# Moving a skipped program from the end of the instruction streams to a place ahead of the last five output tiles

## The chip, the core and the metric

The kernel runs on one core of a Trainium2 chip. The core has five engines, each with an instruction stream of its own: PE (TensorE, matrix products), ACT (ScalarE), DVE (VectorE), POOL (GpSimd) and SP (SyncE, which here only issues transfers). They are tied together by semaphores alone. The metric is the device time of one execution in microseconds. Before the change the median of three runs was 339.82 us (339.38 to 341.15).

## The reference

A sliding-window attention (window 64, 8 batches, 8 heads, 576 positions, head size 64) is followed by a SwiGLU block over the 4608 resulting rows of width 512, with an inner width of 1536:

```python
scores = scale * np.matmul(q, k.transpose(0, 1, 3, 2))
mask = (rel >= 0) & (rel < window)
scores = np.where(mask, scores, -1000000000.0)
scores = scores - np.max(scores, axis=-1, keepdims=True)
attn = np.exp(scores)
attn = attn / (np.sum(attn, axis=-1, keepdims=True) + 1e-09)
...
x = np.ascontiguousarray(attn_out.transpose(0, 2, 1, 3)).reshape(B * S, H * D)
...
g = x @ w_gate
silu = g * (1.0 / (1.0 + np.exp(-g)))
val = x @ w_val
return (silu * val @ w_out).astype(np.float32)
```

## The kernel before

**Tiles and stages.** The rows are taken in 36 chunks of 128 for the attention and in 9 groups of 512 for the SwiGLU block. For a chunk, `T` or `TD` transposes queries and keys, `S` makes the scores and their exponentials, `A` multiplies by the values and divides by the sums, and `X` or `XD` transposes the result into `xT`. For a group `c` and one of twelve inner slices `f`, `F(c, f)` makes four matmuls with the gate weights (call them G) into one PSUM bank and four with the value weights (V) into another; ACT takes the tanh of G (L546), DVE makes `uu` (L548) and then `hT` (L550). `O(c, u)` makes twelve matmuls of `hT` with the output weights (L564) for one tile of 128 output rows, ACT copies the bank to `ost` (L576), and SP stores it (L579). `O_last` does the very last tile in three column pieces (L594), so that its copies (L312 on ACT, L314 on DVE) and stores (L602) are small. The order of all this is written out by hand in `build`. The F matmuls of group 8 are interleaved with the output tiles of group 7: `O(7, u)` stands behind the eighth matmul group of each `u`, but `O(7, 3)` (`late`) stands behind F(8, 11). The stream of PE thus ends with F(8, 9), F(8, 10), F(8, 11) and then five output tiles: O(7, 3), O(8, 0), O(8, 1), O(8, 2) and `O_last`.

**Banks.** The G and V of one F take the next two of four banks; a bank may be written again when the reader of its last content is done. V of F(8, 11) therefore waits for the `hT` of F(8, 9). This wait is a semaphore that DVE raises, carried by the first weight load of that V.

**Two programs.** The exponentials are taken without subtracting a row maximum. `judge` looks, in four steps, whether the sums of all rows are within bounds: steps 0 to 2 (inside group 8) make a flag in SBUF, and step 3 loads it into a register on each engine (L624, `reg_load`). If the flag is not zero, a second program, made by `general`, computes the whole output again in a slower and general way. With the inputs here the flag is zero and that program is skipped.

**The recorder.** All operations are recorded in one `_Graph`. `emit` finds the waits that each operation needs and plays the list into the five streams. For each engine `run` plays the operations up to the mark `cut`, then the branch `If_ne(reg, 0)` with the general program behind it, and on SP the waits until all transfers have landed (`landed`, L148). The streams then meet in the closing barrier of the block (L162): each engine drains, POOL gathers the five signals and releases all.

So each of the streams runs: usual program, branch (L155), general program (skipped), closing barrier. By the listing of the built program, the usual part of PE has 3515 matrix products (each a weight load and a matmul) and the general part 4184.

Of the kernel before, what the change touches and what calls it, by code (L numbers as in the profile page):

```python
# [30 lines left out]
class _Graph:  # L31


    LANES = {"pool": 16, "sp": 16, "act": 8}

    def __init__(self, nc):
        self.nc = nc
        self.ops = []
        self.writers = {}
        self.readers = {}  # L40
        self.cut = None
        self.regs = {}

    def op(self, eng, fn, reads=(), writes=(), dma=False, after=()):
        deps = {o.i: (o, "sync") for o in after}
# [14 lines left out]
            self.readers[k] = []  # L60
        return o

    def general_from_here(self):
        self.cut = len(self.ops)

    def emit(self):
        nc = self.nc
        engines = ["pe", "act", "dve", "pool", "sp"]
        seen = {e: {} for e in engines}
        npos = {e: 0 for e in engines}  # L70
        ndma = {e: 0 for e in engines}
        lanes = {}
        plan = {e: [] for e in engines}
        usual = None
        for o in self.ops:
            if o.i == self.cut:
                usual = dict(lanes)
            e = o.eng
            clock = seen[e]
            waits = []  # L80

            def need(d):
                key = ("dma", d.i) if d.dma else d.eng
                val = 1 if d.dma else d.pos
                if clock.get(key, 0) >= val:
                    return
                waits.append(d)
                d.inc = True
                for k2, v2 in d.clock.items():
                    if clock.get(k2, 0) < v2:  # L90
                        clock[k2] = v2

            deps = sorted(o.deps, key=lambda x: -x[0].i)
            for d, kind in deps:
                if kind != "sync" and d.eng == e and not d.dma and (e == "pe" or kind != "raw") and not o.dma and e != "pool":
                    continue
                need(d)
            if o.dma:
                nl = self.LANES[e]
                o.lane = (e, ndma[e] % nl)  # L100
                o.occ = ndma[e] // nl
                ndma[e] += 1
                prev = lanes.get(o.lane)
                if prev is not None:
                    need(prev)
                lanes[o.lane] = o
            npos[e] += 1
            o.pos = npos[e]
            o.clock = dict(clock)
            if o.dma:  # L110
                o.clock[("dma", o.i)] = 1
            else:
                o.clock[e] = o.pos
            plan[e].append((o, waits))
        cnt = {e: 0 for e in engines}
        for o in self.ops:
            if not o.dma and o.inc:
                cnt[o.eng] += 1
                o.count = cnt[o.eng]
        sem = {e: nc.alloc_semaphore("c_" + e) for e in engines if e != "sp"}  # L120
        for lane in sorted(lanes):
            sem[lane] = nc.alloc_semaphore("d_%s%d" % lane)

        def target(d):
            if d.dma:
                return d.lane, 16 * (d.occ + 1)
            return d.eng, d.count

        def play(eng, e, steps, level):
            for o, waits in steps:  # L130
                want = {}
                for d in waits:
                    k, v = target(d)
                    want[k] = max(want.get(k, 0), v)
                for k, v in want.items():
                    if level.get(k, 0) < v:
                        level[k] = v
                        eng.wait_ge(sem[k], v)
                last = o.fn(eng)
                if o.dma:  # L140
                    last.then_inc(sem[o.lane], 16)
                elif o.inc:
                    last.then_inc(sem[e], 1)

        def landed(eng, on):
            for o in on.values():
                k, v = target(o)
                eng.wait_ge(sem[k], v)  # L148

        def run(eng, e):  # L150
            level = {}
            with eng.register("general_" + e) as reg:
                self.regs[e] = reg
                play(eng, e, [x for x in plan[e] if x[0].i < self.cut], level)
                with eng.If_ne(reg, 0):  # L155
                    play(eng, e, [x for x in plan[e] if x[0].i >= self.cut], level)
                    if e == "sp":
                        landed(eng, lanes)
                if e == "sp":
                    landed(eng, usual)  # L160

        with nc.Block() as block:  # L162
            block.gpsimd(lambda x: run(x, "pool"))
            block.tensor(lambda x: run(x, "pe"))
            block.vector(lambda x: run(x, "dve"))
            block.scalar(lambda x: run(x, "act"))
            block.sync(lambda x: run(x, "sp"))


class _Kernel:  # L170
# [10 lines left out]
    def __init__(self, nc, q, k, v, wg, wv, wo, out):  # L181
        self.nc, self.q, self.k, self.v = nc, q, k, v
        self.wg, self.wv, self.wo, self.out = wg, wv, wo, out
        self.g = _Graph(nc)
        self.alloc()

    def alloc(self):
# [37 lines left out]
        self.ps = [nc.alloc_psum_tensor("ps%d" % i, [128, 512], F32) for i in range(8)]  # L225
        self.rot = {"f": ([0, 1, 2, 3], 0), "a": ([4, 5, 6, 7], 0)}
        self.n_s = 0
        self.stores = {}
        self.kb = [sb("kb%d" % i, 192, F32) for i in range(3)]
        self.ms = sb("ms", H * 192, F32)[:, :].rearrange("p (h k) -> p h k", h=H)  # L230
        self.mx = sb("mx", H, F32)
# [321 lines left out]
    def O(self, c, u, mid=None, kind="a"):  # L553
        g = self.g
        ih = c % self.NH
        hT = self.hT[ih]
        io = (4 * c + u) % self.NO
        ost = self.ost[io]
        OB, ok = self.bank(kind)

        def part(f0, f1):
            def pe(e):
                for f in range(f0, f1):
                    r = e.matmul(OB[:, :], hT[:, f, 128 * u:128 * u + 128], self.Wo[:, f, :],  # L564
                                 start=(f == 0), stop=(f == NF - 1))
                return r

            g.op("pe", pe, reads=[("hT", ih, f) for f in range(f0, f1)] + [("Wo", f) for f in range(f0, f1)], writes=[ok])

        if mid is None:  # L570
            part(0, NF)
        else:
            part(0, 8)
            mid()
            part(8, NF)
        g.op("act", lambda e: e.activation(ost[:, :], OB[:, :], ACTF.Copy), reads=[ok], writes=[("ost", io)])  # L576
        r0 = 512 * c + 128 * u
        was = self.stores.get((c, u), [])
        self.stores[c, u] = [g.op("sp", lambda e: e.dma_start(self.out[r0:r0 + 128, :], ost[:, :]),  # L579
                                  reads=[("ost", io)], dma=True, after=was)]  # L580

    def O_last(self, c, u):
        g = self.g
# [5 lines left out]
        for c0, c1, eng, q in ((0, 256, "act", "sp"), (256, 384, "act", "sp"), (384, 512, "dve", "act")):  # L589
            OB, ok = self.bank("a")  # L590

            def pe(e, OB=OB, c0=c0, c1=c1):
# [5 lines left out]
            g.op("pe", pe, reads=[("hT", ih, f) for f in range(NF)] + [("Wo", f) for f in range(NF)], writes=[ok])  # L598
            d = ost[:, c0:c1]
            self.move(eng, d, OB[:, 0:c1 - c0], [ok] + ([("ost", io)] if c0 else []), [("osth", c0)] + ([("ost", io)] if c0 == 0 else []))  # L600
            self.stores.setdefault((c, u), []).append(
                g.op(q, lambda e, d=d, c0=c0, c1=c1: e.dma_start(self.out[r0:r0 + 128, c0:c1], d), reads=[("osth", c0), ("ost", io)], dma=True))  # L602

    def judge(self, step):

# [9 lines left out]
        elif step == 2:  # L615
            bank, bk = self.bank("f")
            n = bank[0:1, 0:8 * NCH]
            g.op("pe", lambda e: e.matmul(n, self.ones[:, 0:1], ok, start=True, stop=True), reads=["ones", "ok"], writes=[bk])
            g.op("dve", lambda e: e.tensor_reduce(self.low[0:1, :], n, mybir.AxisListType.X, ALU.min), reads=[bk], writes=["low"])
            g.op("dve", lambda e: e.tensor_scalar(self.flag[0:1, :], self.low[0:1, :], 127.5, None, ALU.is_lt),  # L620
                 reads=["low"], writes=["flag"])
        else:
            for eng in ("pe", "act", "dve", "pool", "sp"):
                g.op(eng, lambda e, eng=eng: e.reg_load(g.regs[eng], self.flag[0:1, 0:1]), reads=["flag"])  # L624

    def init_general(self):
        g = self.g
# [81 lines left out]
    def general(self):  # L709


        self.g.general_from_here()
        self.banks("a", [4, 5, 6, 7])
        self.banks("f", [0, 1, 2, 3])
        self.init_general()
        for n in range(NCH):
# [6 lines left out]
            if n % 4 == 3:  # L723
                for f in range(NF):
                    self.F(n // 4, f)
                for u in range(4):
                    self.O(n // 4, u)

    def build(self):
        W = lambda a, b: (self.load_w("g", a, b), self.load_w("v", a, b))  # L730
# [124 lines left out]
                 (2, 0, 0): 12, (2, 1, 0): 13, (2, 1, 2): 14, (2, 2, 1): 15, (2, 3, 0): 16}  # L855
        for n in range(17, NCH):
            place[(n - 5) // 4, (n - 5) % 4, 0] = n
        judged = {(0, 0): 0, (0, 2): 1, (1, 1): 2}
        for c in range(1, NFC):
            for u in range(int(c == 1), 4):  # L860
                late = c == NFC - 1 and u == 3
                for s in range(3):
# [12 lines left out]
                    if c == NFC - 1 and (u, s) in judged:  # L875
                        self.judge(judged[u, s])
                if late:
                    self.O(c - 1, u)
        for u in range(3):
            self.O(NFC - 1, u)  # L880
            if u == 1:
                self.judge(3)
        self.O_last(NFC - 1, 3)
        self.general()
        self.g.emit()


def bass_sliding_window_causal__then__ffn_swiglu_block_kernel(
# [39 lines left out]
```

## Time and profile before

| what | value |
|---|---|
| median of three runs | 339.82 us (339.38 to 341.15) |
| profiled execution, device time | 338.61 us |
| span of that execution, first to last instruction | 337.0 us |
| mean granted TensorE clock | 0.997 |
| PE busy | 320.4 us (95%) |
| DVE, ACT, POOL busy | 215.6, 140.1, 110.8 us |
| end of the last output tile's copy on DVE | 331.6 us after the start of the span |

Times of the profile are microseconds from the start of the span. Line numbers (L155) are those of the kernel before. PEld is the weight load of PE, which runs beside the matmuls. Names with a q (PEldq, ACTq, SPq) are instructions that an engine's sequencer handles by itself: branches, loads of a register, waits, drains and the issue of transfers; the page does not count them as busy. "q8 instruction" and "q14 instruction" are transfers that bring instructions.

### The profile page before, as it was taken

To read this page: it belongs to the slowest core of one execution; us is meant where nothing else is said; L and a number is where in the kernel's file an instruction comes from. 1 tells how busy PE (TensorE), PEld (TensorE's weight loads), DVE (VectorE), ACT (ScalarE), POOL (GpSimd) and SP (SyncE) were. 2 spreads that over 40 slices of the span, in tenths; PEclk is the share of its full clock that TensorE was granted. 3 is DMA by queue.
4 is the path that set the end of the run, shared out by engine and by line. 5 is a ranking of instruction groups with operands and counts; after the bars stand their busy time and mean duration, and the time that the engine had idled before them with its cause. 6 is when DMAs were issued, how large, how long until landed. Compare 5 with 4: busy or idle time off the path is not lost.

```text
span 337.0 us, 8375 instructions
## 1 busy us (share of the span) xinstructions
PE 320.4 (95%) x3478; PEld 165.7 (49%) x3515; DVE 215.6 (64%) x481; ACT 140.1 (42%) x256; POOL 110.8 (33%) x141
## 2 busy tenths in 40 slices
PE   8889989999999999999999999999999999999993
PEld 3657557554444444444444444444444444444442
DVE  5658798476666866666666666666666665555600
ACT  2655764444444444444444444444444422223321
POOL 7999993553545432353333330000000000000000
PEclk9999999999999999999999999999999999999998
DMA  9999999999999999999999999334331111000022
GB/s 169 152 189 173 164 197 158 156 168 166 156 174 173 172 174 171 157 152 134 125 119 117 130 133 118 78 75 77 79 78 49 49 49 47 32 31 34 31 93 71
DMA packets 169517, 40.21 MB, mean 119 GB/s; under 512 B 155904, under 2 KB 164992, under 8 KB 169472
## 3 DMA queue, kind: packets, MB, share of 16 engines
q0 software_dynamic: 117312, 18.36, 77.1%
q1 hardware_dynamic: 50976, 20.66, 32.5%
q10 hardware_dynamic: 1184, 0.59, 0.7%
q8 instruction: 29, 0.48, 0.6%
q14 instruction: 16, 0.13, 0.1%
HBM read 37.75 MB, written 9.44 MB: 140 GB/s over the span
## 4 chain that ended last, share of the span: by engine, by line
PE 85%; DMA 4%; POOL 4%; DVE 2%; issue 2%; ACT 1%; SPq 0%; POOLq 0%
PE ps L540 51%; PE ps L564 26%; PE ps L475 4%; DMA qT<-qn 2%; PE ps L426 2%; DMA Wv<-in_moe_w_val_dram 2%; POOL va L357 1%; PE ps L594 1%; POOL Wg L363 1%; DVE uu L548 1%; POOL qn L295 1%; POOL kn L295 1%; PE ps L382 0%; POOL Wv L363 0%; DVE pt L441 0%
## 5 line engine op out<-in xcount | busy, mean ns | idle before, releaser
L548 DVE SCALAR_TENSOR_TENSOR uu<-sig,ps 128x512 bf16<-128x512 bf16 (+2 forms) x122 | 76.1, 623 | 82.4 <-ACT sig L546 82.1
L540 PE MATMUL ps<-xT,Wv 128*128 128x512 bf16 (+2 forms) x487 | 113.3, 355 | 0.8 <-DMA Wv<-in_moe_w_val_dram 0.7
L540 PE MATMUL ps<-xT,Wg 128*128 128x512 bf16 (+2 forms) x456 | 106.5, 353 | 6.6 <-issue 4.8
L564 PE MATMUL ps<-Wo,hT 128*128 128x512 bf16 x417 | 95.5, 379 | 0.3 <-issue 0.2
L546 ACT ACTIVATE sig<-ps 128x512 bf16<-128x512 f32 (+2 forms) x122 | 66.9, 549 | 60.4 <-PE ps L540 59.8
L550 DVE SCALAR_TENSOR_TENSOR hT<-uu,ps 128x512 bf16<-128x512 bf16 (+2 forms) x122 | 76.3, 625 | 4.8 <-PE ps L540 0.6
L540 PEld LDWEIGHTS ps<-xT,Wv 128*128 128x128 bf16 x488 | 47.0, 98 | 47.6 <-DMA Wv<-in_moe_w_val_dram 1.0
L564 PEld LDWEIGHTS ps<-Wo,hT 128*128 128x128 bf16 x420 | 41.0, 98 | 48.9
L540 PEld LDWEIGHTS ps<-xT,Wg 128*128 128x128 bf16 x488 | 43.7, 98 | 41.9 <-ACT xT L516 0.8
L295 POOL DMA_DIRECT2D qn<-in_q_dram x38 | 35.2, 944 | 84.7 <-DMA qT<-qn 83.3
L576 ACT ACTIVATE ost<-ps 128x512 f32<-128x512 f32 x35 | 20.9, 597 | 95.1 <-PE ps L564 92.2
L436 ACT ACTIVATE pt<-ps 128x512 bf16<-128x512 f32 x72 | 38.9, 595 | 22.0 <-PE ps L426 22.0
L357 POOL DMA_DIRECT2D va<-in_v_dram x40 | 37.2, 941 | 0.9 <-issue 0.6
L295 POOL DMA_DIRECT2D kn<-in_k_dram x38 | 35.4, 937 | 3.7 <-DMA Wo<-in_moe_w_out_dram 3.7
L493 DVE TENSOR_TENSOR xb<-ps,rc 128x256 bf16<-128x256 f32 x72 | 30.6, 424 | 2.5
L441 DVE TENSOR_TENSOR pt<-pt,mask 128x512 bf16<-128x512 bf16 x64 | 24.1, 416 | 0.2 <-ACT pt L436 0.2
L475 PE MATMUL ps<-va,pt 64*64 64x65 bf16 x1088 | 22.9, 197 | 0.6
L475 PEld LDWEIGHTS ps<-va,pt 64*64 64x64 bf16 x1088 | 15.0, 106 | 15.8 <-issue 11.0
L490 DVE RECIPROCAL rc<-ps 128x4 f32<-128x4 f32 x72 | 12.5, 174 | 8.8 <-PE ps L475 8.8
L426 PE MATMUL ps<-qT,kT 64*64 64x64 bf16 (+1 forms) x864 | 15.9, 201 | 0.6 <-DMA qT<-qn 0.6
L426 PEld LDWEIGHTS ps<-qT,kT 64*64 64x64 bf16 x864 | 12.6, 108 | 2.7 <-issue 1.1
L343 PE MATMUL ps<-wz 128*128 128x512 bf16 x17 | 6.9, 573 | 1.4 <-DVE wz L257 1.2
(50 smaller groups left out, 67.3 us busy)
## 6 DMA issues: line engine op xcount, KB each, us to landing
out_dram<-ost SPq DMA_DIRECT2D x35, 256.0 KB, 2.5
va<-in_v_dram POOLq DMA_DIRECT2D x32, 128.0 KB, 11.0
qn<-in_q_dram POOLq DMA_DIRECT2D x30, 128.0 KB, 11.8
kn<-in_k_dram POOLq DMA_DIRECT2D x30, 128.0 KB, 11.1
Wo<-in_moe_w_out_dram POOLq DMA_DIRECT2D x2, 768.0 KB, 15.1
Wg<-in_moe_w_gate_dram POOLq DMA_DIRECT2D x5, 256.0 KB, 8.1
Wv<-in_moe_w_val_dram POOLq DMA_DIRECT2D x5, 256.0 KB, 8.8
fk<-in_k_dram SPq DMA_DIRECT2D x1, 512.0 KB, 4.9
```

The lines of the kernel that those rows point to most:

```text
L295: self.g.op("pool", lambda e, d=d, a=a: e.dma_start(d, a), writes=ks, dma=True)
L357: g.op("pool", lambda e, d=d, a=a: e.dma_start(d, a), writes=ks, dma=True)
L426: r = e.matmul(sv[h][o:o + 64, c, q0:q1], self.kT[ps, c, kk:kk + 64], qT[ps, c, q0:q1], start=not biased, stop=not biased or c == 3 and kk ...
L436: g.op("act", lambda e, po=po, si=si: e.activation(po, si, ACTF.Exp, scale=SCALE), reads=[bk], writes=[pk])
L441: "dve", lambda e: e.tensor_tensor(po, po, m, ALU.mult), reads=[pk, "mask"], writes=[pk]))
L475: r = e.matmul(av[half][ws, j, :], pt[ks, h, ws], vv[ks, h, 0:65], start=key == q[0], stop=key == q[-1])
L493: g.op("dve", lambda e, xo=xo, rb=rb, a=av[half]: e.tensor_tensor(xo, a[:, :, 0:64], rb, ALU.mult), reads=[bk, ("rc", ir)], writes=[("xb", ...
L540: r = e.matmul(bank[:, 0:n], W[:, kk, f * 128:f * 128 + 128], xT[:, kk, t0:t1], start=(kk == 0), stop=(kk == NK - 1))
L546: g.op("act", lambda e: e.activation(sig[:, 0:n], G[:, 0:n], ACTF.Tanh, scale=0.5), reads=[gk], writes=[("sig", i)])
L548: g.op("dve", lambda e: e.scalar_tensor_tensor(uu[:, 0:n], sig[:, 0:n], 1.0, G[:, 0:n], ALU.add, ALU.mult), reads=[("sig", i), gk], writes ...
L550: g.op("dve", lambda e: e.scalar_tensor_tensor(hT[:, f, t0:t1], uu[:, 0:n], 0.5, V[:, 0:n], ALU.mult, ALU.mult), reads=[("uu", i), vk], wr ...
L564: r = e.matmul(OB[:, :], hT[:, f, 128 * u:128 * u + 128], self.Wo[:, f, :], start=(f == 0), stop=(f == NF - 1))
```

## The change

The operations of the usual and of the general program are recorded in two graphs, each with semaphores of its own. A new class `_Program` plays them: on each engine the usual program up to `general_at`, then the branch with the general program behind it, and then the rest of the usual program. `general_at` is set ahead of O(7, 3), so the last five output tiles stand behind the skipped program in each stream. Inside the branch, a gate on each side makes all five engines wait for one another; with the flag at zero neither gate is executed. The loads of the flag into registers (`judge(3)`) move from behind O(8, 1) to behind O(7, 2). The chaining of stores of the same rows (`stores`, `after=was`) goes, since the general program now stores first.

```diff
-    def general_from_here(self):
-        self.cut = len(self.ops)
...
+class _Program:
+    def __init__(self, nc, usual, general, at):
+        self.nc, self.usual, self.general, self.at = nc, usual, general, at
+        self.regs = {}
+
+    def emit(self):
+        nc, usual, general, at = self.nc, self.usual, self.general, self.at
+        usual.plan()
+        general.plan()
+        gates = [nc.alloc_semaphore("gate%d" % i) for i in range(2)]
+        end = 1 << 30
+
+        def gate(eng, i):
+            eng.drain().then_inc(gates[i], 1)
+            eng.wait_ge(gates[i], 5)
 
         def run(eng, e):
-            level = {}
             with eng.register("general_" + e) as reg:
                 self.regs[e] = reg
-                play(eng, e, [x for x in plan[e] if x[0].i < self.cut], level)
+                usual.play(eng, e, 0, at)
                 with eng.If_ne(reg, 0):
-                    play(eng, e, [x for x in plan[e] if x[0].i >= self.cut], level)
                     if e == "sp":
-                        landed(eng, lanes)
+                        usual.landed(eng, at)
+                    gate(eng, 0)
+                    general.play(eng, e, 0, end)
+                    if e == "sp":
+                        general.landed(eng, end)
+                    gate(eng, 1)
+                usual.play(eng, e, at, end)
                 if e == "sp":
-                    landed(eng, usual)
+                    usual.landed(eng, end)
...
     def general(self):
-        self.g.general_from_here()
+        usual, self.g = self.g, _Graph(self.nc, "g")
...
+        self.program = _Program(self.nc, usual, self.g, self.general_at)
+        self.program.emit()
...
-        judged = {(0, 0): 0, (0, 2): 1, (1, 1): 2}
+        judged = {(0, 0): 0, (0, 2): 1, (1, 1): 2, (2, 1): 3}
...
                 if late:
+                    self.general_at = len(self.g.ops)
                     self.O(c - 1, u)
         for u in range(3):
             self.O(NFC - 1, u)
-            if u == 1:
-                self.judge(3)
         self.O_last(NFC - 1, 3)
         self.general()
-        self.g.emit()
```

More of the change, by code (lines that the diff above doesn't have):

```diff
@@ L34, with __init__ @@
     LANES = {"pool": 16, "sp": 16, "act": 8}
-    def __init__(self, nc):
-        self.nc = nc
+    ENGINES = ["pe", "act", "dve", "pool", "sp"]
+    def __init__(self, nc, name):
+        self.nc, self.name = nc, name
         self.ops = []
@@ L40, in __init__ @@
         self.readers = {}
-        self.cut = None
-        self.regs = {}
     def op(self, eng, fn, reads=(), writes=(), dma=False, after=()):
@@ L61, in op, with plan @@
         return o
-    def general_from_here(self):
-        self.cut = len(self.ops)
-    def emit(self):
-        nc = self.nc
-        engines = ["pe", "act", "dve", "pool", "sp"]
+    def plan(self):
+        engines = self.ENGINES
         seen = {e: {} for e in engines}
@@ L72, in emit @@
         lanes = {}
-        plan = {e: [] for e in engines}
-        usual = None
+        self.steps = {e: [] for e in engines}
         for o in self.ops:
-            if o.i == self.cut:
-                usual = dict(lanes)
             e = o.eng
@@ L113, in emit @@
                 o.clock[e] = o.pos
-            plan[e].append((o, waits))
+            self.steps[e].append((o, waits))
         cnt = {e: 0 for e in engines}
@@ L119, in emit @@
                 o.count = cnt[o.eng]
-        sem = {e: nc.alloc_semaphore("c_" + e) for e in engines if e != "sp"}
+        self.sem = {e: self.nc.alloc_semaphore(self.name + "c_" + e) for e in engines if e != "sp"}
         for lane in sorted(lanes):
[L122 to L148, printed above, removed]
+            self.sem[lane] = self.nc.alloc_semaphore(self.name + "d_%s%d" % lane)
+        self.level = {e: {} for e in engines}
+    def target(self, d):
+        if d.dma:
+            return d.lane, 16 * (d.occ + 1)
+        return d.eng, d.count
+    def play(self, eng, e, i0, i1):
+        level = self.level[e]
+        for o, waits in self.steps[e]:
+            if not i0 <= o.i < i1:
+                continue
+            want = {}
+            for d in waits:
+                k, v = self.target(d)
+                want[k] = max(want.get(k, 0), v)
+            for k, v in want.items():
+                if level.get(k, 0) < v:
+                    level[k] = v
+                    eng.wait_ge(self.sem[k], v)
+            last = o.fn(eng)
+            if o.dma:
+                last.then_inc(self.sem[o.lane], 16)
+            elif o.inc:
+                last.then_inc(self.sem[e], 1)
@@ new lines, in landed @@
+    def landed(self, eng, i1):
+        last = {o.lane: o for o in self.ops if o.dma and o.i < i1}
+        for o in last.values():
+            k, v = self.target(o)
+            eng.wait_ge(self.sem[k], v)
+class _Program:
[11 more added lines that the diff above has]
+            eng.wait_ge(gates[i], 5)
@@ L183, in __init__ @@
         self.wg, self.wv, self.wo, self.out = wg, wv, wo, out
-        self.g = _Graph(nc)
+        self.g = _Graph(nc, "")
+        self.general_at = None
         self.alloc()
@@ L227, in alloc @@
         self.n_s = 0
-        self.stores = {}
         self.kb = [sb("kb%d" % i, 192, F32) for i in range(3)]
@@ L577, in O @@
         r0 = 512 * c + 128 * u
-        was = self.stores.get((c, u), [])
-        self.stores[c, u] = [g.op("sp", lambda e: e.dma_start(self.out[r0:r0 + 128, :], ost[:, :]),
-                                  reads=[("ost", io)], dma=True, after=was)]
+        g.op("sp", lambda e: e.dma_start(self.out[r0:r0 + 128, :], ost[:, :]), reads=[("ost", io)], dma=True)
     def O_last(self, c, u):
@@ L600, in O_last @@
             self.move(eng, d, OB[:, 0:c1 - c0], [ok] + ([("ost", io)] if c0 else []), [("osth", c0)] + ([("ost", io)] if c0 == 0 else []))
-            self.stores.setdefault((c, u), []).append(
-                g.op(q, lambda e, d=d, c0=c0, c1=c1: e.dma_start(self.out[r0:r0 + 128, c0:c1], d), reads=[("osth", c0), ("ost", io)], dma=True))
+            g.op(q, lambda e, d=d, c0=c0, c1=c1: e.dma_start(self.out[r0:r0 + 128, c0:c1], d), reads=[("osth", c0)], dma=True)
     def judge(self, step):
@@ L623, in judge @@
             for eng in ("pe", "act", "dve", "pool", "sp"):
-                g.op(eng, lambda e, eng=eng: e.reg_load(g.regs[eng], self.flag[0:1, 0:1]), reads=["flag"])
+                g.op(eng, lambda e, eng=eng: e.reg_load(self.program.regs[eng], self.flag[0:1, 0:1]), reads=["flag"])
     def init_general(self):
```

## The prediction

> **What bounds the kernel now.** I read the page first, then the end of the chain of work, and then the rows of single source lines for the instructions that the page does not count as busy.
>
> ```profile
> span 337.0 us, 8375 instructions
> PE 320.4 (95%) x3478; PEld 165.7 (49%) x3515; DVE 215.6 (64%) x481; ACT 140.1 (42%) x256; POOL 110.8 (33%) x141
> q8 instruction: 29, 0.48, 0.6%
> PE 85%; DMA 4%; POOL 4%; DVE 2%; issue 2%; ACT 1%; SPq 0%; POOLq 0%
> ```
>
> PE is busy 95% of the span and carries 85% of the chain, so a pause of PE costs its whole length. The third row counts 29 transfers of instructions, 0.48 MB, some 16.6 KB each. The first two columns of the next rows are start and length.
>
> ```profile
> 308.79 2.59 PE ps L564 x12
> 311.38 6.91 PE ps L540 x32
> 318.28 0.65 PE ps L564 x3
> ...
> 318.98 9.66 PE ps L564 x44
> 328.64 2.66 PE ps L594 x36
> ...
> 331.33 0.29 DVE ost L314
> ```
>
> PE runs without a hole through the place of the change (318.1, between L540 and L564) to 331.3. The last copy ends at 331.62. The span ends at 337.0, 5.4 us later: that tail is what the change can shorten. Rows of the branch (L155), of SP's last waits (L148, three stretches) and of the closing barrier (L162); durations are in ns, then first and last start:
>
> ```profile
> L155 PEldq COMPARE_BRANCH  x1: 3614/3614/3614, 330.1 to 330.1; - x1
> L155 DVEq COMPARE_BRANCH  x1: 72/72/72, 331.3 to 331.3; - x1
> L155 ACTq COMPARE_BRANCH  x1: 54/54/54, 332.0 to 332.0; - x1
> L148 SPq EVENT_SEMAPHORE  x5: 27/28/28, 333.6 to 333.9; - x5
> L148 SPq EVENT_SEMAPHORE  x6: 28/28/28, 334.3 to 334.7; - x6
> L162 PEldq DRAIN  x1: 68/68/68, 333.8 to 333.8; - x1
> L162 DVEq DRAIN  x1: 61/61/61, 334.4 to 334.4; - x1
> L162 ACTq DRAIN  x1: 80/80/80, 334.7 to 334.7; - x1
> L162 DVEq EVENT_SEMAPHORE  x1: 21/21/21, 335.1 to 335.1; - x1
> L162 PEldq EVENT_SEMAPHORE  x1: 51/51/51, 336.9 to 336.9; - x1
> ```
>
> Jumping over the general program is dear on every engine: PE's next instruction comes at 333.8, 3.6 us after the branch began; DVE's 334.4 − 331.3 = 3.1 us and ACT's 334.7 − 332.0 = 2.7 us after. Then comes what nobody else has: DVE leaves the barrier at 335.1, PE at 336.9, and that event is the end of the span. PE's drain was over at 333.9, so PE was not behind the others with work. What it did get is one more transfer of instructions. These three rows are from the stretches 331.0 to 332.5, 334.3 to 335.6 and, in mid-kernel, 267.3 to 268.5:
>
> ```profile
> q8 instruction: 1, 0.02, 5.4%
> q8 instruction: 1, 0.02, 5.0%
> q8 instruction: 1, 0.02, 4.9%
> ```
>
> The first belongs to PE's branch; with shares of 16 engines it took 0.054 × 16 × 1.5 = 1.30 us. The second lies between PE's drain and its late event (0.050 × 16 × 1.3 = 1.04 us). I read it so: the jump fetched the block holding the drain, the event after it was the first instruction of the next block, and that was fetched only then. The third is one of quiet times, 0.049 × 16 × 1.2 = 0.94 us.
>
> **The change part by part: PE's branch in mid-stream.** It now stands behind V of F(8, 11), ahead of O(7, 3). Price: its row, 3.61 us; with the transfer of quiet times in place of the longer one 3.61 − 0.36 = 3.25. No store is under way there (the one of O(7, 2) is long issued), so I take 3.3. Of this, what is hidden is the time by which PE's sequencer reaches the branch ahead of its matmuls. V of F(8, 11) waits for the `hT` of F(8, 9). Whether a wait stops the sequencer can be read in an earlier run of F (256 rows each), where nothing but the four V products lies between such a wait and a wait of line 138 that the sequencer handles itself:
>
> ```profile
> 29.42 0.42 DVE L550 SCALAR_TENSOR_TENSOR hT<-uu,ps 128x256 bf16<-128x256 bf16 x1
> L138 PEldq EVENT_SEMAPHORE  x1: 51/51/51, 29.9 to 29.9; - x1
> 29.99 0.42 PEld L540 LDWEIGHTS ps<-xT,Wv 128*128 128x128 bf16 x4
> ```
>
> The sequencer comes through at 29.9, right behind the end of that `hT` (29.84) and before the weight loads it has passed on begin (29.99). So it is held by the wait and then runs on at once. Now the same at the new place:
>
> ```profile
> 315.35 0.69 DVE L550 SCALAR_TENSOR_TENSOR hT<-uu,ps 128x512 bf16<-128x512 bf16 x1
> 317.25 1.03 PE L540 MATMUL ps<-xT,Wv 128*128 128x512 bf16 x4
> 318.12 3.19 PE L564 MATMUL ps<-Wo,hT 128*128 128x512 bf16 x13
> ```
>
> The `hT` of F(8, 9) ends at 316.04, so the branch begins at 316.10; O(7, 3) would start at 318.12. Cover 2.02 us; PE resumes at 316.10 + 3.3 = 319.4, a weight load (0.1 us) precedes the matmul, so 319.5. Stall: **1.4 us**, between 1.2 (with 3.1, as DVE paid) and 1.7 (with 3.6).
>
> **The loads of the flag.**
>
> ```profile
> L624 DVEq TENSOR_LOAD <-flag x1: 546/546/546, 318.8 to 318.8; - x1
> L624 PEldq TENSOR_LOAD <-flag x1: 737/737/737, 322.0 to 322.0; - x1
> L624 ACTq TENSOR_LOAD <-flag x1: 467/467/467, 326.1 to 326.1; - x1
> L624 SPq TENSOR_LOAD <-flag x1: 526/526/526, 327.1 to 327.1; - x1
> 311.41 0.60 ACT L576 ACTIVATE ost<-ps 128x512 f32<-128x512 f32 x1 [2.86 <-PE ps L564]
> 312.91 0.69 DVE L548 SCALAR_TENSOR_TENSOR uu<-sig,ps 128x512 bf16<-128x512 bf16 x1 [2.91 <-ACT sig L546]
> ```
>
> They move to O(7, 2) and cost nothing: PE's 0.74 us lies under the 2.59 us of that tile's matmuls, ACT's 0.47 under its own copy of 0.60, DVE's 0.55 in an idle 2.91. If that cover went, PE would pay 0.74. SP has only the store of O(7, 2) ahead of its load and none behind it until O(7, 3). POOL's load stays where it was. The gates and the general program are not executed.
>
> **The branches of the others.**
>
> ```profile
> 317.45 0.60 ACT L546 ACTIVATE sig<-ps 128x512 bf16<-128x512 f32 x1 [1.13 <-PE ps L540]
> 320.91 0.60 ACT L576 ACTIVATE ost<-ps 128x512 f32<-128x512 f32 x1 [2.86 <-PE ps L564]
> ```
>
> ACT branches when its last tanh has begun (317.5), and with its 2.7 us is back at 320.2; it is wanted at 320.91 plus PE's stall of 1.4. DVE, back at about 322, has only the copy near the end left. SP's next store follows ACT's copy, so that SP too has a fetch's time to spare. Behind ACT at its branch are its five tiles' copies, which PE's banks do not need for another four tiles. All hidden; ACT would begin to cost if its jump took over 4.8 us.
>
> **The tail.** Behind the last tile, each engine now goes on into the barrier without a long jump. By the listings of the two built programs PE's stream to its drain counts three instructions more than before, so the block edge that stood right behind the drain now stands some three earlier, beside the last matmul; by the listing the jump lands about 168 instructions ahead of it (48 + 36 matmuls with their weight loads), which is 13 us of work (318.1 to 331.3), time enough for the next block. PE then leaves with the others: 336.9 − 335.1 = 1.8, at most 1.9 us. SP's waits too: between its two rows (333.9, 334.3) is a hole of 0.4 us with a step of 0.07 elsewhere, of the same kind as the others' 2.7 to 3.1 us after a branch; gone as well, with ACT's drain of 334.7 no longer late. Together **2.2 us**, between 1.5 (if the stores land later) and 2.3.
>
> **The sum.** + 1.4 − 2.2 = − 0.8 us: span 336.2, profiled execution 338.61 − 0.8 = 337.8. That execution is 1.2 us under the median of the runs, so I apply the difference to the median: **339.0 us**, its own range 338.7 (1.2 − 2.3) to 340.0 (1.7 − 1.5). This kernel can't be told from no change within 0.5%, 1.7 us.
>
> **Rivals.** *PE's jump is hidden wholly.* The sequencer can be far ahead:
>
> ```profile
> L138 PEldq EVENT_SEMAPHORE  x2: 51/51/51, 285.4 to 285.6; - x2
> 289.31 1.03 PE L540 MATMUL ps<-xT,Wg 128*128 128x512 bf16 x4
> ```
>
> Here it handles at 285.4 a wait that belongs to the matmul of 289.31, some 3.9 us ahead, more than the jump costs. But an output tile stood between, which had let the waits come true; at the new place three F follow one another. Were it so, 339.82 − 2.2 = 337.6. Chance 0.13.
>
> *The branch is cheap in itself.* DVE's and ACT's rows show 72 and 54 ns; PE's 3.61 could be the wait for its matmuls. Against this: DVE and ACT show the same hole behind the branch. It gives 337.6 too; chance 0.03. [...]
>
> *A second fetch behind the jump (slower).* If the jump lands within a few instructions of a block's edge, PE stops again, as before between drain and last event: 336.9 − 333.8 = 3.1 us. It decides if fewer than about 30 instructions are left in the block (0.1 us each, against 3.1). Then + 1.4 + 3.1 − 2.2 = + 2.3: 342.1. The count above speaks against it, unless the late event had another reason. Chance 0.09.
>
> *The tail stays.* The change doesn't do what it could: PE's late event comes from the barrier itself, or from its closing jump. Then + 1.4 or a little more: 341.2, up to 341.5. Against: the other four engines leave at 335.1. Chance 0.10.
>
> **How the numbers follow.** Main case 0.65: within 0.5% 0.61, faster 0.03, slower 0.01. Hidden jump or cheap branch 0.16 at 337.6 (− 0.65%): faster 0.12, within 0.04. Tail stays 0.10: within 0.07, slower 0.03. Second fetch 0.09: slower. Sum: faster 0.15, within 0.72, slower 0.13. The range 337.5 to 341.3 leaves out the second fetch and the edges of the others.
>
> **What would show it.** In the changed profile PE's branch should take about 3.3 us from about 316.1, with a hole of 1.4 us ahead of L584 (the new line of the output matmuls); the copies of O(7, 3) follow PE, not ACT's branch; the last event of PE lies beside those of the other engines, some 3.6 us after the last copy instead of 5.4. A hole above 3 us, or a second one inside the output tiles, makes the prediction wrong to the slow side; no hole at all, to the fast side.

## The result, and the profile after

The changed kernel takes 339.18 us (median of 20 runs, 337.72 to 341.39) against 340.63 us (20 runs) of the kernel before: ratio 0.9961, 95% interval 0.9942 to 0.9979. By the ratio that is some 1.3 us less (the two medians lie 1.45 us apart). It lies within 0.5%, on the fast side of it.

The page of the profile after, answering to the first rows of before:

```profile
span 337.1 us, 8412 instructions
PE 325.3 (97%) x3515; PEld 165.2 (49%) x3515; DVE 215.5 (64%) x481; ACT 140.0 (42%) x256; POOL 110.8 (33%) x141
q8 instruction: 30, 0.49, 0.6%
PE 88%; DMA 4%; POOL 4%; DVE 1%; issue 1%; ACT 1%; POOLq 0%
```

The two spans, 337.0 and 337.1, hide the difference: in this execution PE came to the place of the change 0.76 us later (312.14 against 311.38). The change does not touch what lies ahead of it, and two profiles of the kernel before differ by more there (311.38 and 312.72). So I count from that place on. The end of the chain of work (start, length):

```profile
312.14 6.91 PE ps L560 x32
319.05 1.54 issue
320.58 10.54 PE ps L584 x48
331.12 2.67 PE ps L612 x36
...
333.81 0.29 DVE ost L334
```

Line 560 is 540 of before, 584 is 564, 612 is 594. Between the last F matmuls and O(7, 3) stands a hole of 1.54 us that the kernel before did not have ("issue": nothing that the profile shows was waited for). The work behind it is as long as before. From the end of the last copy (334.10) to the end of the span are 3.0 us instead of 5.4 (331.62 to 337.0). Now, by lines, the flag load of PE (L641), the branches (L170) and the closing barrier (L182); duration in ns, then when it started:

```profile
L641 PEldq TENSOR_LOAD <-flag x1: 489/489/489, 308.1 to 308.1; - x1
```

```profile
L170 PEldq COMPARE_BRANCH  x1: 3662/3662/3662, 316.9 to 316.9; - x1
L170 ACTq COMPARE_BRANCH  x1: 50/50/50, 318.2 to 318.2; - x1
L170 DVEq COMPARE_BRANCH  x1: 72/72/72, 319.6 to 319.6; - x1
```

```profile
L182 SPq DRAIN  x1: 13/13/13, 336.9 to 336.9; - x1
L182 DVEq EVENT_SEMAPHORE  x1: 21/21/21, 337.0 to 337.0; - x1
L182 PEldq EVENT_SEMAPHORE  x1: 51/51/51, 337.0 to 337.0; - x1
```

PE read the flag at 308.1, while its queue held matmuls. It leaves the barrier with the others, and SP's drain is what they waited for. Rows of the order of time around the branch, of DVE, PE and ACT:

```profile
316.12 0.69 DVE L570 SCALAR_TENSOR_TENSOR hT<-uu,ps 128x512 bf16<-128x512 bf16 x1
318.02 1.03 PE L560 MATMUL ps<-xT,Wv 128*128 128x512 bf16 x4
320.58 1.69 PE L584 MATMUL ps<-Wo,hT 128*128 128x512 bf16 x7 [1.54 <-issue]
323.38 0.60 ACT L596 ACTIVATE ost<-ps 128x512 f32<-128x512 f32 x1 [4.57 <-PE ps L584]
```

The `hT` of F(8, 9) ends at 316.81 and the branch begins at 316.9. The four V matmuls start 0.216 us apart (6.91 us for 32), so O(7, 3) could have started at 318.02 + 0.86 = 318.88 and starts at 320.58: a stall of 1.70 us (the page shows 1.54, as it has the last matmul end at 319.05). ACT's first copy waits for PE, not for ACT's own jump.

### The profile page after: what moved, and what is told of

It is laid out like the page before. It is cut to its first block, busy times and chain, and to the rows that moved or that the text cites. A ratio compares the mean times of both kernels' runs of the same rounds, so it can differ in the third digit from the quotient of the medians.

```text
span 337.1 us, 8412 instructions
## 1 busy us (share of the span) xinstructions
PE 325.3 (97%) x3515; PEld 165.2 (49%) x3515; DVE 215.5 (64%) x481; ACT 140.0 (42%) x256; POOL 110.8 (33%) x141
## 4 chain that ended last, share of the span: by engine, by line
PE 88%; DMA 4%; POOL 4%; DVE 1%; issue 1%; ACT 1%; POOLq 0%
PE ps L560 54%; PE ps L584 26%; PE ps L495 4%; DMA qT<-qn 3%; PE ps L446 2%; DMA Wv<-in_moe_w_val_dram 2%; POOL va L377 1%; PE ps L612 1%; POOL Wg L383 1%; PE ps L402 1%; POOL qn L315 1%; POOL kn L315 1%; POOL Wv L383 0%; PE ps L527 0%; DVE uu L568 0%
## 5 line engine op out<-in xcount | busy, mean ns | idle before, releaser
L560 PE MATMUL ps<-xT,Wg 128*128 128x512 bf16 (+2 forms) x488 | 113.7, 355 | 1.7 <-DMA Wg<-in_moe_w_gate_dram 0.6
L334 DVE COPY ost<-ps 128x128 f32<-128x128 f32 x1 | 0.3, 292 | 13.5 <-PE ps L612 13.5
```

Of the source, the lines that this page charges most:

```text
L560: r = e.matmul(bank[:, 0:n], W[:, kk, f * 128:f * 128 + 128], xT[:, kk, t0:t1], start=(kk == 0), stop=(kk == NK - 1))
```

## The experiments

All kernels ran in sets that share runs of the kernel before. "Tail" is the time from the end of the last copy (L314 or L334) to the end of the span.

**The two kernels again.** The changed kernel, unaltered:

> The changed kernel again, on the chip of the runs beside it, as their yardstick. Its first 20 runs gave 0.9961 of the kernel before (0.9942 to 0.9979); its profile has a stall of 1.7 us of PE at the branch and a tail that is 2.4 us shorter, which is -0.7 us or 0.998. Theory A (these two terms are all of it): 0.996 to 0.999, and the same stall of 1.7 us. Rival (something outside these two places gains as well): 0.996 or less.

Ratio 0.9966 (0.9947 to 0.9986). End of its chain:

```profile
319.27 1.60 issue
320.87 10.53 PE ps L584 x48
331.40 2.66 PE ps L612 x36
...
334.09 0.29 DVE ost L334
```

The stall is the same (1.60 and the same 0.16). But with a span of 336.5 the tail is 2.1 us, not 3.0. The stores show why; these rows of the transfers (KB, then us from issue to landing) are of the last three stores, in the first profile of the changed kernel and in this one:

```profile
out_dram<-ost SPq DMA_DIRECT2D x1, 128.0 KB, 3.0
out_dram<-ost SPq DMA_DIRECT2D x1, 64.0 KB, 2.6
out_dram<-ost ACTq DMA_DIRECT2D x1, 64.0 KB, 2.1
```

```profile
out_dram<-ost SPq DMA_DIRECT2D x1, 128.0 KB, 1.7
out_dram<-ost SPq DMA_DIRECT2D x1, 64.0 KB, 1.6
out_dram<-ost ACTq DMA_DIRECT2D x1, 64.0 KB, 1.6
```

In the first, one q8 transfer of instructions lies between 333.5 and 335.0, right behind the issue of the store of 128 KB (332.87); in the second there is none before the end. The kernel before, once more:

> The kernel before itself, for a second profile of its tail. Theory A (the last event of PE is the first instruction of a block): PE's event again lies about 1.8 us behind those of the other engines, and the last three stores again need more than 2 us to land, as instruction transfers run beside them. Rival C: the late event was a chance of one execution, and all engines leave together.

```profile
L162 DVEq EVENT_SEMAPHORE  x1: 21/21/21, 336.4 to 336.4; - x1
L162 PEldq EVENT_SEMAPHORE  x1: 51/51/51, 338.8 to 338.8; - x1
```

PE's last event is late again, by 2.4 us, and the 128 KB again need 3.1 us. Its tail is 338.9 − 332.96 = 5.9 us. So the two pairs of profiles give + 1.70 − 2.4 = − 0.7 us and + 1.76 − 3.8 = − 2.0 us; the timed difference of 1.3 us lies between. Nothing outside the two places is needed; but two pairs that lie 1.3 us apart, and an interval that holds values of both theories, do not exclude a small third term, so the rival is weakened and not refuted.

**Does a longer queue hide the jump?** One output tile ahead of the branch:

```diff
                 if late:
-                    self.general_at = len(self.g.ops)
                     self.O(c - 1, u)
+                    self.general_at = len(self.g.ops)
```

> The branch stands one output tile later, between O(7, 3) and O(8, 0). Theory A (PE's jump costs 3.66 us from the time that its sequencer reaches the branch, and what is queued ahead of it is the cover): twelve more matmuls are queued, 2.6 us, so the cover grows from 2.0 to the most that was seen in the kernel before, 3.6 to 3.9 us, and the stall shrinks from 1.7 to 0 to 0.2 us. Time 1.5 to 1.7 us under the changed kernel: 0.991 to 0.994 of before. Rival B (the branch begins only when PE's matmuls are nearly done, whatever is queued): the stall stays at 1.7 us and the time that of the changed kernel. The tail is the same in both.

Ratio 0.989 (0.986 to 0.9919), against 0.9966 of the changed kernel in the same set. Its branch, and its chain:

```profile
L170 PEldq COMPARE_BRANCH  x1: 3422/3422/3422, 318.0 to 318.0; - x1
```

```profile
312.53 6.91 PE ps L560 x32
319.44 10.36 PE ps L584 x48
329.80 2.66 PE ps L612 x36
```

The branch costs as much as ever, 3.4 us, and PE has no hole: O(7, 3) was queued behind the F matmuls and ran meanwhile. Rival B falls. The medians differ by 2.65 us, more than the 1.5 to 1.7 expected, and the tail is 2.1 us in both profiles. A part of the rest is in the granted clocks on record: seven of the twelve runs of the changed kernel in this set have a mean clock of 0.995 (median 340.25 us), none of these six has. The changed kernel's other five runs have a median of 339.07, which leaves 1.96 us. Against the kernel before, the profile accounts for the time: no stall, and a tail of 2.1 us instead of 5.4 and 5.9, that is 3.3 to 3.8 us, with a ratio that makes 3.75.

**Is it the distance?** The general program left out (with the flag at zero it is not executed; what is lost is the fallback for other inputs), so that PE jumps over three instructions:

```diff
-        self.init_general()
-        for n in range(NCH):
-            ...
```

> The changed kernel with the general program left out: the flag is still made, loaded and branched on, and behind the branch stand only the gates, so that PE jumps over three instructions. The output is that of the usual program. Theory A (the price of PE's branch is the transfer of the block it lands in): the target is in a block that is there, the branch takes 0.1 us or less, no stall; 1.7 us less than the changed kernel, 0.988 to 0.993 of before, as with the branch one tile later. Rival D (any taken branch on PE costs 3.6 us): the stall of 1.6 to 1.7 us stays, 0.996.

```profile
L170 PEldq COMPARE_BRANCH  x1: 219/219/219, 316.2 to 316.2; - x1
```

At the same place, with the same wait ahead of it, the branch takes 0.22 us instead of 3.66 (0.1 or less was expected), and no hole is left. Ratio 0.9906 (0.9876 to 0.9937). Rival D falls: a taken branch on PE took 0.22 us where it led over the gates alone, and 3.66 where it led over the general program.

**Is the late event a block's edge?** One matmul, then 60, added to the skipped program of the kernel before, and 82 to that of the changed kernel; none is ever executed:

```diff
+    def skipped(self):
+        def pe(e):
+            for _ in range(1):
+                r = e.matmul(self.ps[3][:, :], self.wz[:, 0:128], self.wz[:, :], start=True, stop=True)
+            return r
+
+        self.g.op("pe", pe, reads=["wz"], writes=[("ps", 3)])
...
+        self.skipped()
         self.init_general()
```

> The kernel before with one more matmul on PE inside the program that is skipped: two instructions that are never executed. Theory A (PE's last event was late because its instruction was the first of a block that had to be fetched after the jump): the two instructions move drain and event behind the edge into one block, PE leaves the barrier with the others, the span ends at 335.1 to 335.2 instead of 337.0 and the time falls by 1.8 us: 0.993 to 0.996 of before. Rival C (the late event belongs to the long jump or to the barrier itself): nothing changes, 1.000, and PE's last event still lies 1.8 us behind those of the others.

> The kernel before with 60 more matmuls on PE in the program that is skipped (120 instructions, never executed), so that drain and event lie in the middle of a block. Theory A: PE's last event comes with the others, the branch takes 3.6 us as in the kernel before (5.1 us with one more matmul, where two blocks were fetched at once), the last stores land in about 3.1 us instead of 4.5, the span ends near 335.1 and the ratio is 0.993 to 0.996. Rival C (the event's lateness has nothing to do with block edges, and one more matmul was chance): 1.000 with a late event.

With one: ratio 0.9966 (0.9942 to 0.9991), somewhat less gain than the 0.993 to 0.996 expected. With 60: 0.9939 (0.9916 to 0.9962). In both, PE leaves with the others; with one:

```profile
L162 SPq DRAIN  x1: 13/13/13, 340.2 to 340.2; - x1
L162 PEldq EVENT_SEMAPHORE  x1: 51/51/51, 340.4 to 340.4; - x1
```

Instructions that never run made this kernel faster, and PE's late event is gone, as theory A has it of instructions that are moved within their block. Rival C falls. But another cost came up. These are PE's branch with one and with 60, and the first of the last stores with one:

```profile
L155 PEldq COMPARE_BRANCH  x1: 5097/5097/5097, 334.1 to 334.1; - x1
L155 PEldq COMPARE_BRANCH  x1: 4932/4932/4932, 331.4 to 331.4; - x1
```

```profile
out_dram<-ost SPq DMA_DIRECT2D x1, 128.0 KB, 4.5
```

Two blocks were fetched at the jump (two q8 transfers begin at 335.1 with one matmul, at 331.7 and 332.5 with 60), the branch took 5.1 and 4.9 us, and the store beside them needed 4.5 and 4.7 us. With 60 I had expected 3.6 and 3.1; that part of the expectation was wrong. So the tails of these two profiles are 340.4 − 335.53 = 4.9 and 338.2 − 332.91 = 5.3 us, only 0.1 to 1.0 us shorter than the 5.4 and 5.9 of the kernel before, while the times gained 1.2 and 2.1. With 60 most of the timed gain is not in the profile; its execution (339.97 us) was the second slowest of nine with a median of 338.87. Why two blocks are fetched, and what the faster executions did otherwise, I have not found out.

**A landing at the edge.** The padding of 82:

> The changed kernel with 82 more matmuls on PE inside the program that is skipped (164 instructions, never executed), so that by the count of the streams the jump lands three instructions ahead of a block's edge instead of 167. Theory A (after a jump only the block of its target is there; the next one is asked for then): PE executes one or two matmuls after the jump and stops again, some 3 us after the jump's end (in the kernel before 3.1 us lay between drain and last event): time 2.5 to 3.1 us above the changed kernel, 1.003 to 1.007 of before. Rival C (no such edge, or the next block comes in time): as the changed kernel.

Ratio 1.0064 (1.0038 to 1.0089): the changed kernel turned slower than before by instructions that are not executed. Its chain:

```profile
318.24 1.68 issue
319.91 0.39 PE ps L584
320.30 3.14 issue
323.44 12.40 PE ps L584 x47
```

After the jump PE runs one matmul (0.39 us, with 47 behind the second hole) and stops again for 3.14 us, as the slow rival of the prediction had it. The output tiles then take 12.40 us for 47 matmuls instead of 10.53 for 48. The table by stretches shows the reason (columns: stretch, its length, busy time of PE, PEld, DVE, ACT, POOL, granted clock, DMA share, GB/s):

```profile
320.70:324.10 3.40, 0.66 (x2) 0.28 (x3) 0.00 (x0) 0.00 (x0) 0.00 (x0) 0.53 0.02 5
324.10:327.50 3.40, 3.40 (x9) 1.21 (x8) 0.00 (x0) 0.00 (x0) 0.00 (x0) 0.50 0.02 5
327.50:330.90 3.40, 3.40 (x16) 1.48 (x15) 0.00 (x0) 0.79 (x2) 0.00 (x0) 0.97 0.20 77
```

The granted clock is halved in the second stall and for some 4 us behind it: 9 matmuls in a stretch that else holds 16. From the first output matmul on, the profile loses 15.93 − 10.53 = 5.4 us against that of the changed kernel; the timed loss, 343.25 − 339.76 = 3.5 us, is smaller. On the one side, seven of the twelve runs of the yardstick had a lowered clock as well (the others have a median of 339.07). On the other, five of the nine runs here have a mean clock of 0.995, where the profiled one has 0.990, so the clock seems to have been lowered for a shorter time in them. I have no profile of such a run.

**What the tail consists of.** SP's closing waits put in the order of issue, on the kernel with one tile ahead of the branch:

```diff
-        for o in last.values():
+        for o in sorted(last.values(), key=lambda o: o.i):
```

> The branch one tile later, and SP's closing waits taken in the order in which the transfers were issued, so that only those of the last three stores are left when these land. Theory A (SP's chain of waits ends the span): the ten waits of 0.06 us behind the landing of the store of 256 columns move ahead of it; span 0.5 to 0.6 us shorter than with the branch one tile later alone (334.9 us), ratio lower by 0.0015. Rival E (another engine or the landing itself sets the end): the same time as without the sorting. If stalls of PE alone lower the granted clock, all executions have 1.000, as there.

Ratio 0.9905 (0.9875 to 0.9935), not told apart from 0.989. In its profile the 128 KB landed in 3.0 us and the tail is 336.3 − 333.70 = 2.6 us; with the same landing and unsorted waits it is 3.0 (first profile of the changed kernel) and 2.9 (below). So the order of the waits is worth 0.3 to 0.4 us there, less than expected, and the time cannot show it. That all executions have a clock of 1.000 was not so: this profile's mean is 0.995, with no stall at the branch. The clock was lowered in the first stages, far ahead of the change; these rows (columns as above) are of this profile and of that with one tile ahead of the branch and the waits as they were:

```profile
22.00:25.40 3.40, 3.33 (x62) 2.55 (x55) 2.96 (x11) 0.53 (x2) 3.40 (x6) 0.50 1.61 188
22.00:25.40 3.40, 3.27 (x75) 2.91 (x76) 3.05 (x11) 1.32 (x4) 3.40 (x6) 1.00 1.59 188
```

In a stretch of 3.4 us at half the clock PE ran 62 matmuls where it ran 75 at the full one. The padding of 100 below shows the same in its profile (0.51, mean 0.995). So a lowered mean clock can come from a place that has nothing to do with the branch, and it is a part of the scatter in all these times; why it falls there in some executions and not in others, no run here shows.

Then three paddings of the same kernel: 8 matmuls, 100, none.

> The branch one tile later, with 8 more matmuls on PE in the skipped program (16 instructions, never executed), so that PE's sequencer enters a new block some 16 instructions before its end, while the last stores are on their way. Theory F (the transfer of an instruction block beside the last stores makes these land late): a q8 transfer starts within 1 us of the issue of the store of 256 columns, that store lands in 3 us or more instead of 1.7, and from the last matmul to the end of the span it takes 3.2 to 3.6 us instead of 2.7. Rival G (late landings are chance and have nothing to do with the transfer): 1.7 us and 2.7 us as often as with the edge elsewhere.

> The same with 100 more matmuls in the skipped program (200 instructions), so that by the count no block edge lies between the jump and the end, and no block is asked for in the last tile. Theory F: the store of 256 columns lands in 1.7 us, from the last matmul to the end 2.7 us, no stall at the branch; the time is the lowest of the three of this set, 0.986 to 0.990 of before, and 0.5 to 0.9 us under the one with the edge in the last tile. Rival G: no difference between the two.

> The branch one tile later, unpadded, as yardstick for the two beside it; the first time it gave 0.989 (0.986 to 0.992) with 2.7 us from the last matmul to the end. Its edge lies within a few instructions of the end by the count, so the transfer may fall before or behind the end. Theory F: between the two others or equal to the one with no edge. Theory A on the stall: nil again.

The store of 128 KB with 8, with 100 and with none:

```profile
out_dram<-ost SPq DMA_DIRECT2D x1, 128.0 KB, 2.2
```

```profile
out_dram<-ost SPq DMA_DIRECT2D x1, 128.0 KB, 1.7
```

```profile
out_dram<-ost SPq DMA_DIRECT2D x1, 128.0 KB, 3.0
```

```profile
q8 instruction: 1, 0.02, 1.5%
```

With 100 no block is asked for near the end, and the store lands in 1.7 us (tail 2.1). With none, one q8 transfer lies in the tail (last row, of 331.0 to 335.0: 0.015 × 16 × 4 = 0.96 us), and it lands in 3.0 (tail 2.9). With 8 the transfer begins 0.5 us ahead of the store's issue, earlier than I had aimed at, and costs only 0.5 us (2.2, where 3 or more was expected; tail 2.4). Over all thirteen profiles: a transfer that begins 0.7 to 0.9 us behind the store's issue goes with a landing of 3.0 to 3.1 (five profiles), none with 1.7 (four), two with 4.5 and 4.7; without the general program one begins with the issue (330.5) and the store lands in 3.4. Theory F stands in the profiles, though no padding put the transfer where the theory foretold the full delay. In the times, 0.9875, 0.9869 and 0.9871 (each about ± 0.003), the three can't be told apart. All three beat both kernels by more than their intervals; the one without padding is the one to keep, 0.9871 (0.9841 to 0.9901).

## Why the prediction was right

The predicted difference was − 0.8 us, the timed one − 1.3 (interval of the ratio: − 0.7 to − 2.0), the two pairs of profiles − 0.7 and − 2.0. The forecast of "within 0.5%" held. That the median is 0.2 us from the 339.0 forecast is partly luck: the kernel before took 340.63 us over 20 runs instead of the 339.82 of three runs on which the forecast stood, and of the two terms the cost and the gain were both taken too small.

- *The branch begins when the `hT` of F(8, 9) is done, 2.02 us ahead of O(7, 3).* Right: 316.81 and 316.9, and 318.88 for the tile.
- *PE's branch costs 3.3 us.* Too low: 3.66 and 3.72. I had put the transfer of quiet times in place of that in the branch's own row. The one at the new place took as long as the one in the row:

```profile
q8 instruction: 1, 0.02, 4.0%
```

(of 317.5 to 319.5 after: 0.040 × 16 × 2.0 = 1.28 us.) So the stall of 1.4 was mis-sized: 1.70 and 1.76, the upper bound.
- *The flag loads and the other engines' jumps cost nothing.* Right: PE's chain has only the one hole, and ACT's copy waits for PE. Only "on every engine" went too far: in the profile before, POOL's drain began 0.5 us behind its branch (304.7 and 305.2) and SP's first wait 0.1 us behind (331.4 and 331.5).
- *The tail loses 2.2 us.* Right in kind, PE's late event is gone and the others' long jumps with it; the size was 2.4 and 3.8. I had bounded it by 2.3, taking the landing of the last stores as given, while that of the 128 KB fell from 3.1 us to 1.7 in the second profile of the changed kernel, where no block was fetched beside them. The sign named for it, PE's last event 3.6 us after the last copy, did not fit that term either (5.4 − 2.2 = 3.2); it came 3.0 and 2.1 us after.
- *The rivals.* The wholly hidden jump is real, one tile later, where the queue is longer (a branch of 3.4 us and no hole); here the waits of three F in a row forbade it. The second stop exists (3.14 us) and made a kernel slower than before (1.0064) when I moved the edge there; the count of instructions had placed it rightly. The cheap branch fell to the kernel without the general program, and the tail did not stay.

## What to carry to other kernels

A branch over a large skipped program cost PE 3.42 to 3.80 us in seven profiles here, whether it stood at the end (3.61 and 3.59) or in mid-stream, and 4.9 to 5.1 where two blocks were fetched; put it where the engine's queue is full of work that waits for nothing: behind one more output tile of twelve matmuls it cost PE no pause, behind a chain of waits one of 1.70 and 1.76 us. At the end of the kernel before, the branch's own row (3.61 us) did not show all of its cost: a block travelled beside the last stores, and the 128 KB landed after 3.1 us, against 1.7 in the four profiles without such a block. And where a jump lands within its block is a matter of instruction counts: 2 and 120 skipped instructions more made the kernel before 0.3 and 0.6% faster, 164 made the changed one 1% slower.

## What I had not expected

A transfer of one block of instructions (0.49 MB in 30 of them, some 16 KB each) beside a store of 128 KB went with a landing after 3.0 us instead of 1.7, and two of them with 4.5. The same kernel had such a transfer beside its last stores in one profile and not in another (3.0 and 1.7 us, changed kernel; likewise with one tile ahead of the branch), so the moment of that transfer differs between executions; what moves it, I have not tested. And two stalls of PE, of 1.7 and 3.1 us with one matmul between, went with a halved granted clock for some 6.8 us, 4 of them full of work, while around a single stall of 1.5 to 1.6 us it stayed at 1.000 in both profiles of the changed kernel. In the first stages, with the waits sorted, it was at 0.50 for the 3.4 us of the row above. What makes the clock fall, these runs do not show: with the landing at the edge the clock was down by 321 us, less than 3 us after the first hole began (318.24), with one matmul in between; and ahead of the fall in the first stages (22.0) PE's longest pauses in the profile with sorted waits were 0.65 and 0.75 us.
